# Retention and gated feed-forward on one core: the transposes of three more units by DMA, and one weight slice moved

## The chip, the cores and the metric

The kernel runs on one core of a Trainium2 chip. A core has TensorE (PE, matmuls; PEld is its load of weights), VectorE (DVE), ScalarE (ACT), GpSimd (POOL) and SyncE (SP, which here only issues DMAs), and 16 DMA engines [...]. The metric is the device time of one execution in microseconds (us); lower is better.

## The reference

Two stages. The first is a retention recurrence for 4 batches, 8 heads, 768 positions and a head size of 64; the second is a feed-forward layer with a SiLU on 3072 tokens of width 512 with an inner width of 2048. What is computed is

```python
gamma = 1.0 - 2.0 ** (-5.0 - np.arange(H))
for t in range(S):
    state = gamma[None, :, None, None] * state + np.einsum('bhd,bhe->bhde', k[:, :, t], v[:, :, t])
    y[:, :, t] = scale * np.einsum('bhd,bhde->bhe', q[:, :, t], state)
...
x = np.ascontiguousarray(attn_out.transpose(0, 2, 1, 3)).reshape(B * S, H * D)
h = x @ w_in
g = h * (1.0 / (1.0 + np.exp(-h)))
return g @ w_out
```

## The kernel before

**Units and chunks.** The 768 positions are cut into 6 chunks of 128. A unit is one chunk of one batch (all 8 heads); unit n is chunk n // 4, batch n % 4, so there are 24. Four units make one chunk of x: 512 tokens by 512 features. For each unit `k` and `q` are needed with the positions along the partitions (as loaded: `kf`, `qf`) and with the features along the partitions (`kt`, `qt`): the latter are transposes. `stage_t` (L429) makes them on TensorE, four 128x128 transposes for `k` and four for `q` into PSUM (`kp`, `qp`, L436), which ScalarE copies out (L438). `stage_s` (L446) makes the sums k times v, `stage_a` (L456) the scores from `kt` and `qt`, `stage_y` (L491) the outputs; its second half, the state products, waits for a fence: a `token` written by GpSimd (L377).

**The DMA's way to the transpose.** For units from `FAR` on (17 to 23) `part_t` (L407) has GpSimd copy `q` and `k` into two 16-bit planes each (`qp`, `kp`, L412), `turn_t` (L416) lets SP issue a transposing DMA for each (`qw`, `kw`, L419), and `join_t` (L422) has ScalarE put the 16-bit halves together to `qt` and `kt` (L426).

**Products.** The first matmul of the layer is cut into (c, f): chunk c of x by slice f of 128 inner features. `product_in` (L643) makes it with 12 matmuls of 512 columns: eight into `ha`, four into `hb` (L650), since each factor is split in a high and a low part and one for the cross terms. Then ScalarE takes `ha` out of PSUM (L660), VectorE subtracts `hb` (L665), ScalarE applies the SiLU (L670), and `put_g` has SP write the result `g` to memory (L676). Three PSUM banks `h0` to `h2` go round among the `ha`, `hb` and, in `stage_t`, `kp`. The loop over `steps` (L918) runs the products in a fixed order, with pairs and triples of chunks first, then (2, 3) to (2, 7), the middle slices of chunks 0 and 1, the last four slices of both, (2, 8) to (2, 15), and chunks 3 to 5 slice by slice. The second matmul (L967, L975) follows when all are done.

**Visits.** The attention work is hung between products: `visit(m)` (L594) does for unit m the transposes, for m - 1 the sums and scores, for m - 2 the outputs, and then issues the loads of a unit further on. The list `at` (L906) puts the visits of units 14 to 17 behind the products (1, 15), (2, 9), (2, 11) and (2, 13), later ones behind every fourth product of chunks 3 and 4.

**Lists that defer work.** What is appended to `behind_copy` runs after ScalarE's next L660, what is appended to `behind_next` after VectorE's next L665; `taken_out[0]` is that L665.

**Weights.** The weights come as pairs of 32-bit words. `take_w` (L253) converts one slice: a load on SP, one pass on ScalarE (L196) and six on VectorE (L199 to L217); slices 0 to 15 are of w_in and are split at once into three parts (L120 to L128, with the buffer `wl`), slices 16 to 31 are of w_out and are stored to memory again (`store_w`, L280), read back in chunk 5 (`get_w`, L692) and split there (`w_out`, L700). The list `takes` (L897) says behind which products a slice is taken.

**Late x of chunk 2.** The outputs of chunk 2 are also written to memory, and read back by `late_y` (L583) into `yr` tiles that `late_x` (L588) splits: loads behind (0, 14) and (1, 12), splits behind (1, 12), (1, 14) and (1, 15).

**Order.** The order on TensorE is written out by hand everywhere. After L882 the other queues are ordered by the scheduler of the tile framework from the order of the program, and by `queue(ins)`, which lets what follows be issued after an instruction. A tag with `bufs` n is a set of n buffers; a new tile waits until the last reader of a free one is done. `kt` has 2, `qt` 3, `kf` 3, `qf` 2, `wl` 1.

Of the kernel before, what the change touches and what calls it, by code (L numbers as in the profile page):

```python
# [33 lines left out]
def kernel(  # L34
# [28 lines left out]
    nc = tc.nc  # L63
# [78 lines left out]
    FAR = 4 * B + 1  # L142
    early = {}

    def load(name, n):
        if n >= len(units):
            return
        c, b = units[n]
        src = {"k": k, "q": q, "v": v}[name]
        if n < EARLY:  # L150

            if n not in early:
                early[n] = wpool.tile([128, 3, H, D], FP32, tag=f"w{4 + n}", name=f"kqv_{n}")
            t = early[n][:, "kqv".index(name)]
        else:
            t = ld.tile([128, H, D], FP32, tag=f"{name}f", name=f"{name}f_{n}",
                        bufs=2 if name == "q" else 3)
        nc.sync.dma_start(out=t, in_=src[b, :, ds(c * C, C)].rearrange("h t d -> t h d"))
        kqv[name][n] = t
# [247 lines left out]
    def part_t(n):  # L407

        for name, (p, tag, bufs) in (("q", (ld, "kf", 3)), ("k", (one, "kt", 2))):
            src = kqv[name].pop(n) if name == "q" else kqv[name][n]  # L410
            t = p.tile([128, 2 * H * D], U16, tag=tag, name=f"{name}p_{n}", bufs=bufs)
            nc.gpsimd.tensor_copy(out=t.rearrange("p (w h d) -> p w h d", w=2, h=H),  # L412
                                  in_=src.bitcast(U16).rearrange("p h (d w) -> p w h d", w=2))
# [169 lines left out]
    def late_y(b):  # L583
        tag = ("kt", "qt")[b % 2]
        y_late[b] = one.tile([128, KIN, C], FP32, tag=tag, name=f"yr_{b}", bufs=2 + b % 2)
        nc.sync.dma_start(out=y_late[b], in_=y_dram[b])
# [11 lines left out]
    def halves(m):  # L598
# [22 lines left out]
        if first and m < FAR:  # L621
            scale_k(m)
# [3 lines left out]

        if FAR <= m < len(units):
            with queue(fenced[0]):
                part_t(m)
        for name in "kqv":  # L630
            for n in (m + 1, m + 2):
                if n >= EARLY and n == (m + 1 if name == "v" or n > FAR else m + 2):
                    load(name, n)
# [6 lines left out]

    pending = []
# [258 lines left out]
    takes += [(0, NF - 2), (2, half), (2, half + 2), (2, half + 4)]  # L900
    takes += [(3, f) for f in (0, 3, 7, 11, 14)]
    takes += [(4, f) for f in (3, 7, 11, 14)]
    takes += [(5, f) for f in (2, 5, 8)]
# [4 lines left out]
    for i, x in enumerate(at):  # L908
# [7 lines left out]
    far = {steps.index(x): EARLY + 6 + i for i, x in enumerate(at)  # L916
           if FAR <= EARLY + 6 + i < len(units)}
    for n, (c, f) in enumerate(steps):  # L918
        if n - 2 in far:
            behind_next.append(lambda m=far[n - 2]: scale_k(m))  # L920
        if n - 3 in far:
            behind_copy.append(lambda m=far[n - 3]: [join_t(name, m) for name in "qk"])
# [6 lines left out]
        if n - 1 in far:  # L929
            turn_t(far[n - 1])  # L930
# [96 lines left out]
```

## Time and profile before

| | |
|---|---|
| median of 3 runs | 623.08 us (619.96 to 623.37) |
| the profiled execution | 619.42 us, span 617.6 us |
| TensorE busy | 603.8 us (98%) |
| VectorE, ScalarE busy | 422.9 us (68%), 313.0 us (51%) |
| GpSimd busy | 22.6 us (4%) |
| DMA queue of SP | 101.21 MB, 57.5% of 16 engines |

The span runs from the first to the last instruction of the trace. Busy shares are means over stages that differ: the first 97 us hold the early visits with little else to fill TensorE, then come products with and without visits up to 352 us, then the second matmul.

```profile
q1 hardware_dynamic: 135056, 101.21, 57.5%
HBM read 66.06 MB, written 36.70 MB: 166 GB/s over the span
L501 PE MATMUL y<-qt,mid 64*64 64x64 f32 x384 | 20.2, 224 | 1.0 <-POOL token L377 1.0
```

The first line gives packets, MB and the share of the 16 engines for SP's queue, the third a group of instructions: what it writes and reads, how many, busy time, mean duration, and the idle time before them with what ended it.

### The profile page before, as it was taken

To read this page: it belongs to the slowest core of one execution; us is meant where nothing else is said; L and a number is where in the kernel's file an instruction comes from. 1 tells how busy PE (TensorE), PEld (TensorE's weight loads), DVE (VectorE), ACT (ScalarE), POOL (GpSimd) and SP (SyncE) were. 2 spreads that over 40 slices of the span, in tenths; PEclk is the share of its full clock that TensorE was granted. 3 is DMA by queue.
4 is the path that set the end of the run, shared out by engine and by line. 5 is a ranking of instruction groups with operands and counts; after the bars stand their busy time and mean duration, and the time that the engine had idled before them with its cause. 6 is when DMAs were issued, how large, how long until landed. Compare 5 with 4: busy or idle time off the path is not lost.

```text
span 617.6 us, 13494 instructions
## 1 busy us (share of the span) xinstructions
PE 603.8 (98%) x5384; PEld 497.5 (81%) x5384; DVE 422.9 (68%) x731; ACT 313.0 (51%) x595; POOL 22.6 (4%) x79
## 2 busy tenths in 40 slices
PE   6899999999999999999999999999999999999997
PEld 5777887888888888888788888888888888888886
DVE  4998889899789877676699773635545453654631
ACT  6678896676654667766587732312221221412311
POOL 3000000000001111120000000000000000000000
PEclk9999999999999999999999999999999999999999
DMA  9989896464677999989767542533524433442301
GB/s 191 225 203 228 243 240 200 157 198 157 222 177 208 259 255 239 259 223 282 255 230 248 203 139 68 171 102 100 173 69 134 140 103 102 141 132 89 116 1 68
DMA packets 137999, 107.31 MB, mean 174 GB/s; under 512 B 94801, under 2 KB 103249, under 8 KB 137937
## 3 DMA queue, kind: packets, MB, share of 16 engines
q1 hardware_dynamic: 135056, 101.21, 57.5%
q10 hardware_dynamic: 2880, 5.24, 2.3%
q8 instruction: 42, 0.69, 0.5%
q14 instruction: 21, 0.16, 0.1%
HBM read 66.06 MB, written 36.70 MB: 166 GB/s over the span
## 4 chain that ended last, share of the span: by engine, by line
PE 84%; DVE 0%; DVEq 0%; issue 0%; POOLq 0%
PE ha L650 25%; PE o L967 21%; PE oa L967 14%; PE hb L650 12%; PE ob L967 7%; PE y L501 2%; PE sc L462 1%; PE sc L452 1%; PE o L975 0%; PE oa L975 0%; PE qp L436 0%; PE kp L436 0%; PE ob L975 0%; DVE o L993 0%; DVEq L1022 0%
## 5 line engine op out<-in xcount | busy, mean ns | idle before, releaser
L650 PE MATMUL ha<-xt,wi 128*128 128x512 f32 x768 | 193.8, 394 | 1.3 <-ACT xt L557 0.7
L650 PEld LDWEIGHTS ha<-xt,wi 128*128 128x128 f32 x768 | 141.9, 188 | 33.6 <-ACT wi L126 1.2
L967 PE MATMUL o<-wo,gs 128*128 128x512 f32 x564 | 143.2, 389 | 0.0
L717 DVE TENSOR_TENSOR gs<-gr,gs 128x512 fp32r<-128x512 f32 x96 | 62.1, 685 | 90.3 <-ACT gs L715 90.3
L967 PEld LDWEIGHTS o<-wo,gs 128*128 128x128 f32 x564 | 105.9, 188 | 21.9
L715 ACT ACTIVATE gs<-gr 128x512 fp32r<-128x512 f32 x96 | 53.6, 621 | 134.2 <-issue 131.8
L967 PE MATMUL oa<-wo,gs 128*128 128x512 f32 x376 | 115.8, 389 | 0.0
L650 PE MATMUL hb<-xt,wi 128*128 128x512 f32 x384 | 102.9, 390 | 0.0
L665 DVE TENSOR_TENSOR g<-g,hb 128x512 f32<-128x512 f32 x96 | 65.6, 683 | 42.0 <-ACT g L660 26.3
L650 PEld LDWEIGHTS hb<-xt,wi 128*128 128x128 f32 x384 | 71.8, 188 | 15.5 <-DVE g L665 0.2
L670 ACT ACTIVATE g<-g 128x512 f32<-128x512 f32 x96 | 60.3, 628 | 47.1 <-DVE g L665 47.1
L967 PEld LDWEIGHTS oa<-wo,gs 128*128 128x128 f32 x376 | 70.6, 188 | 14.7
L967 PE MATMUL ob<-wo,gs 128*128 128x512 f32 x188 | 73.7, 392 | 0.0
L660 ACT ACTIVATE g<-ha 128x512 f32<-128x512 f32 x96 | 57.0, 594 | 31.9 <-PE ha L650 15.1
L718 DVE SCALAR_TENSOR_TENSOR gs<-gs 128x512 fp32r<-128x512 f32 x96 | 62.0, 683 | 0.0
L967 PEld LDWEIGHTS ob<-wo,gs 128*128 128x128 f32 x188 | 35.3, 188 | 8.7 <-DVE o L985 1.6
L196 ACT ACTIVATE ca<-wf 128x512 f32<-128x512 f32 x32 | 21.4, 668 | 6.0 <-DVE cw L217 5.5
L212 DVE SCALAR_TENSOR_TENSOR ca<-wf,ca 128x512 f32<-128x512 uint32 x32 | 22.7, 710 | 0.5
L984 ACT ACTIVATE o<-o 128x512 f32<-128x512 f32 x10 | 6.0, 600 | 33.4 <-PE o L967 33.0
L206 DVE SCALAR_TENSOR_TENSOR cs<-ca,cs 128x512 uint32<-128x512 uint32 x32 | 22.1, 691 | 0.9
L501 PE MATMUL y<-qt,mid 64*64 64x64 f32 x384 | 20.2, 224 | 1.0 <-POOL token L377 1.0
L470 DVE TENSOR_TENSOR am<-sc,decay 128x512 f32<-128x512 f32 x24 | 16.5, 687 | 6.6 <-PE sc L462 6.5
(93 smaller groups left out, 562.0 us busy)
## 6 DMA issues: line engine op xcount, KB each, us to landing
gd<-g SPq DMA_DIRECT2D x96, 256.0 KB, 3.1
gr<-gd SPq DMA_DIRECT2D x96, 256.0 KB, 2.7
wf<-in_moe_w_out_dram SPq DMA_DIRECT2D x16, 512.0 KB, 4.2
out_dram<-o ACTq DMA_DIRECT2D x20, 256.0 KB, 2.1
wf<-in_moe_w_in_dram SPq DMA_DIRECT2D x16, 256.0 KB, 4.2
wf<-in_moe_w_in_dram SPq DMA_DIRECT2D x32, 128.0 KB, 4.0
kf<-in_k_dram SPq DMA_DIRECT2D x16, 256.0 KB, 5.1
qf<-in_q_dram SPq DMA_DIRECT2D x16, 256.0 KB, 4.0
```

The source lines that it names most:

```text
L196: nc.scalar.activation(out=a.bitcast(FP32), in_=hi.bitcast(FP32), func=AF.Abs, scale=65536.0)
L206: nc.vector.scalar_tensor_tensor(out=s, in0=a, scalar=3, in1=s, op0=ALU.logical_shift_left, op1=ALU.bitwise_or)
L212: nc.vector.scalar_tensor_tensor(out=p.bitcast(FP32), in0=lo, scalar=2.0 ** -52, in1=p.bitcast(FP32), op0=ALU.mult, op1=ALU.mult)
L501: i = nc.tensor.matmul(yp[ts(e, D), o, a, :], lhsT=lhsT, rhs=rhs, start=(e, o) not in started, stop=True, skip_group_check=True).ins
L650: nc.tensor.matmul(hb if i == 2 else ha, lhsT=w_sb[f][:, i, ts(kk, 128)], rhs=xt[c][:, i, kk, :], start=kk == 0 and i != 1, stop=kk == KIN ...
L660: copied[:] = [nc.scalar.activation(out=hs, in_=ha, func=AF.Copy, scale=ONE_E).ins]
L665: taken_out[:] = [nc.vector.tensor_tensor(out=hs, in0=hs, in1=hb, op=ALU.subtract).ins]
L670: nc.scalar.activation(out=hs, in_=hs, func=AF.Silu)
L715: nc.scalar.activation(out=t[:, 0, :], in_=g, func=AF.Copy, scale=HALF)
L717: nc.vector.tensor_tensor(out=t[:, 1, :], in0=g, in1=high, op=ALU.subtract)
L718: nc.vector.scalar_tensor_tensor(out=t[:, 2, :], in0=t[:, 1, :].bitcast(FP32), scalar=-1.0 / EPS, in1=high, op0=ALU.mult, op1=ALU.add)
L967: nc.tensor.matmul(o, lhsT=g, rhs=wo[f][:, i, :], start=f == 0 and i != 1, stop=f == NF - 1 and i != 0)
```

## The change

Three things. `FAR` becomes 14, so units 14 to 16 also leave `stage_t`: they are parted, turned and joined (`LATER`, 17, is where the old rhythm begins). Unit 14 is parted in the product (2, 3), turned after (2, 5), joined in (2, 8); units 15 and 16 are parted one visit ahead, turned a product after that, and joined in (2, 10) and (2, 12), where the old rhythm parts a unit in its own visit and joins it three products later. The loads of `k` and `q` of unit 15 and of `q` of 16 get places of their own (`apart`, `loads_at`), and `k` of 16 goes to `wl`; those of `k` and `q` of 17 are issued one visit later. The odd `late_y` tiles go to `wl` in place of `qt`. And the entry (2, 8) leaves the list of takes while (5, 0) joins it, so that the w_out slices after the first are each taken one place later, the thirteenth at (5, 0).

```diff
--- before.py
+++ after.py
@@ -139,7 +139,8 @@
     kqv = {"k": {}, "q": {}, "v": {}}
     EARLY = 2 * B
 
-    FAR = 4 * B + 1
+    FAR = 3 * B + 2
+    LATER = 4 * B + 1
     early = {}
 
     def load(name, n):
@@ -147,6 +148,11 @@
             return
         c, b = units[n]
         src = {"k": k, "q": q, "v": v}[name]
+        if n == LATER - 1 and name == "k":
+            t = conv.tile([128, H, D], FP32, tag="wl", name=f"kf_{n}")
+            nc.sync.dma_start(out=t, in_=src[b, :, ds(c * C, C)].rearrange("h t d -> t h d"))
+            kqv[name][n] = t
+            return
         if n < EARLY:
 
             if n not in early:
@@ -404,13 +410,17 @@
 
     planes, turned = {}, {}
 
-    def part_t(n):
+    def part_t(n, after=None):
 
         for name, (p, tag, bufs) in (("q", (ld, "kf", 3)), ("k", (one, "kt", 2))):
             src = kqv[name].pop(n) if name == "q" else kqv[name][n]
             t = p.tile([128, 2 * H * D], U16, tag=tag, name=f"{name}p_{n}", bufs=bufs)
-            nc.gpsimd.tensor_copy(out=t.rearrange("p (w h d) -> p w h d", w=2, h=H),
-                                  in_=src.bitcast(U16).rearrange("p h (d w) -> p w h d", w=2))
+            i = nc.gpsimd.tensor_copy(
+                out=t.rearrange("p (w h d) -> p w h d", w=2, h=H),
+                in_=src.bitcast(U16).rearrange("p h (d w) -> p w h d", w=2)).ins
+            if after is not None:
+                tc.add_manual_dep(i, after.name, mybir.DependencyInfo(
+                    mybir.DependencyClass.Sync, mybir.DependencyReason.DATA), reason="later")
             planes[name, n] = t
 
     def turn_t(n):
@@ -581,8 +591,8 @@
     y_late = {}
 
     def late_y(b):
-        tag = ("kt", "qt")[b % 2]
-        y_late[b] = one.tile([128, KIN, C], FP32, tag=tag, name=f"yr_{b}", bufs=2 + b % 2)
+        p, tag, bufs = ((one, "kt", 2), (conv, "wl", 1))[b % 2]
+        y_late[b] = p.tile([128, KIN, C], FP32, tag=tag, name=f"yr_{b}", bufs=bufs)
         nc.sync.dma_start(out=y_late[b], in_=y_dram[b])
 
     def late_x(b):
@@ -618,18 +628,20 @@
             if m > 3 * B + 1 and units[m - 1][1] == B - 1:
 
                 behind_copy.append(next_chunk)
-        if first and m < FAR:
+        if first and m < LATER:
             scale_k(m)
         if last:
             states_with(1)
             finish_y(m - 2, yp)
 
-        if FAR <= m < len(units):
+        n = m if m >= LATER else m + 1
+        if FAR < n < len(units) and (m < LATER - 1 or m >= LATER):
             with queue(fenced[0]):
-                part_t(m)
+                part_t(n)
         for name in "kqv":
             for n in (m + 1, m + 2):
-                if n >= EARLY and n == (m + 1 if name == "v" or n > FAR else m + 2):
+                if (n, name) not in apart and n >= EARLY and n == (
+                        m + 1 if name == "v" or n >= LATER else m + 2):
                     load(name, n)
         if EARLY + 2 <= m < 3 * B + 2:
             with queue(masked[0]):
@@ -638,6 +650,7 @@
                     begin_w()
 
 
+    apart = [(FAR + 1, "k"), (FAR + 1, "q"), (FAR + 2, "q")]
     pending = []
 
     def product_in(c, f):
@@ -897,10 +910,10 @@
     takes = [(1, 5)] + [(0, f) for f in range(6, half)]
     takes += [(2, half - 4), (2, half - 2)]
     takes += [(0, half), (0, half + 3), (1, half + 1), (1, half + 3)]
-    takes += [(0, NF - 2), (2, half), (2, half + 2), (2, half + 4)]
+    takes += [(0, NF - 2), (2, half + 2), (2, half + 4)]
     takes += [(3, f) for f in (0, 3, 7, 11, 14)]
     takes += [(4, f) for f in (3, 7, 11, 14)]
-    takes += [(5, f) for f in (2, 5, 8)]
+    takes += [(5, f) for f in (0, 2, 5, 8)]
     behind = {x: lambda: next(half_visits) for x in pairs[:-1]}
     behind[pairs[-1]] = lambda: [visit(3 * B + 1), behind_next.append(end_w)]
     at = ([(1, NF - 1)] + [(2, f) for f in range(NF - 7, NF - 2, 2)] +
@@ -913,21 +926,32 @@
     behind[1, NF - 1] = lambda: [late_x(3), visit(EARLY + 6)]
 
 
-    far = {steps.index(x): EARLY + 6 + i for i, x in enumerate(at)
-           if FAR <= EARLY + 6 + i < len(units)}
+    far = {m: steps.index(x) for m, x in enumerate(at, EARLY + 6)}
+    first_far = steps.index((2, 3))
+    parts = {first_far: FAR}
+    turns_at = {first_far + 2: FAR, far[FAR] + 1: FAR + 1, far[FAR + 1] + 1: FAR + 2}
+    joins_at = {far[m] + 1: m for m in range(FAR, LATER)}
+    for m in range(LATER, len(units)):
+        turns_at[far[m] + 1], joins_at[far[m] + 3] = m, m
+    scales_at = {far[m] + 2: m for m in range(LATER, len(units))}
+    loads_at = {first_far + 4: [("k", FAR + 1), ("q", FAR + 1)], far[FAR] + 1: [("q", FAR + 2)]}
     for n, (c, f) in enumerate(steps):
-        if n - 2 in far:
-            behind_next.append(lambda m=far[n - 2]: scale_k(m))
-        if n - 3 in far:
-            behind_copy.append(lambda m=far[n - 3]: [join_t(name, m) for name in "qk"])
+        if n in scales_at:
+            behind_next.append(lambda m=scales_at[n]: scale_k(m))
+        if n in joins_at:
+            behind_copy.append(lambda m=joins_at[n]: [join_t(name, m) for name in "qk"])
+        if n in parts:
+            behind_next.append(lambda m=parts[n]: part_t(m, taken_out[0]))
         product_in(c, f)
         put_g(1)
         store_w()
         if (c, f) in takes:
             take_w(taken_out[0], n < len(pairs + three))
         behind.get((c, f), lambda: None)()
-        if n - 1 in far:
-            turn_t(far[n - 1])
+        if n in turns_at:
+            turn_t(turns_at[n])
+        for name, m in loads_at.get(n, ()):
+            load(name, m)
         if c == NC - 1:
             if f == 0:
                 for i in range(W_READ):
```

## The prediction

> **What bounds the kernel now.** The head of the page first: which engine is full, and where.
>
> ```profile
> PE 603.8 (98%) x5384; PEld 497.5 (81%) x5384; DVE 422.9 (68%) x731; ACT 313.0 (51%) x595; POOL 22.6 (4%) x79
> ...
> PE   6899999999999999999999999999999999999997
> PEclk9999999999999999999999999999999999999999
> ```
>
> TensorE is busy for 98% of the span, and from the fourth slice on the row shows nothing but nines, at full granted clock. A busy row alone doesn't prove a bound, so the next view is what TensorE waited for after 97 us:
>
> ```profile
> PE ha L650 <- ACT wi L126: 0.4, 1, 0.4
> PE y L501 <- POOL token L377: 0.3, 1, 0.3
> ```
>
> That is 0.7 us in 520. So after the first 97 us the end is set by the number and length of TensorE's own instructions; other engines matter only once they become so late that it waits. The chain of waits gives each instruction's share of the path. Columns: start, length, what. First the visit of unit 16 (with transposes), then that of unit 17, which has its transposes from the DMA already:
>
> ```profile
> 187.45 0.44 PE kp L436 x4
> 187.89 0.44 PE qp L436 x4
> 188.33 0.86 PE y L501 x48
> ...
> 190.12 0.23 PE y L501 x16
> 190.35 2.04 PE ha L650 x8
> ...
> 196.02 0.86 PE y L501 x48
> 196.88 0.47 PE sc L452 x32
> 197.34 0.47 PE sc L462 x32
> 197.81 0.23 PE y L501 x16
> 198.04 2.04 PE ha L650 x8
> ```
>
> Both visits do the same work from `y` to the last `y` (0.86 + 0.47 + 0.47 + 0.23 = 2.03 us); that of unit 16 has 0.44 + 0.44 us of transposes before it. The whole visits are 190.35 - 187.45 = 2.90 and 198.04 - 196.02 = 2.02 us, so a unit's eight transposes cost 0.88 us of path. The groups give `kp` 276 and `qp` 273 ns each, 2.2 us a unit; those are latencies that overlap, so the chain is the row to price with.
>
> [...] beside unit 17's copy (1504 ns instead of a median 1051) two VectorE operations took 1.41 us each in place of 0.69. [...] here `kw` lands in a median 3.6 us, plain `kf` loads in 5.1.
>
> **The change part by part.** *Transposes of units 14 to 16 leave TensorE.* 3 x 0.88 = 2.6 us off the path. The clean length of a product stays 2.72 us (1.81 + 0.91). Nothing else on TensorE changes. Gain 2.6 us.
>
> *What takes their place.* Per unit two GpSimd copies, two DMA transposes on SP, two 16-bit joins on ScalarE in place of two PSUM copies.
>
> ```profile
> L426 ACT COPY kt<-kw 128x1024 uint16<-128x1024 uint16 x7 | 9.5, 1353 | 0.1
> L438 ACT COPY kt<-kp 128x512 f32<-128x512 f32 x17 | 9.8, 577 | 2.4 <-PE kp L436 2.4
> ```
>
> ```profile
> kw<-kp SPq DMA_TRANSPOSE x7, 3.6
> ```
>
> ScalarE: 2 x (1.36 - 0.58) = 1.55 us more a unit. Is there room? The windows from visit to visit (columns: length, busy PE, PEld, DVE, ACT, POOL, clock, DMA share, GB/s):
>
> ```profile
> 170.32:178.89 8.57, 8.57 (x162) 7.32 (x161) 6.95 (x14) 5.34 (x10) 0.09 (x1) 1.00 0.67 157
> 178.89:187.45 8.56, 8.56 (x162) 7.32 (x161) 7.93 (x16) 4.60 (x8) 0.09 (x1) 1.00 0.84 230
> 187.45:196.02 8.57, 8.57 (x165) 7.10 (x165) 7.94 (x16) 5.64 (x12) 0.09 (x1) 1.00 0.76 230
> ```
>
> Each window shrinks to 8.56 - 0.88 = 7.7 us. ScalarE becomes 6.9, 6.2, 7.2: it fits. DMA: a transpose is 256 KB like a load, and a load's 1024 packets of 18 ns are 1.15 us of the 16 engines (estimate: the same for a transpose). The loads of `k`, `q`, `v` are also spread otherwise, and I count about 7 us in each window: 90%, like the 0.93 of later windows where TensorE doesn't wait. VectorE: a `w_out` slice is 0.42 + 0.42 + 0.69 + 0.42 + 0.71 + 0.73 = 3.4 us. The slice that leaves (2, 8) ran from 177.5 to 182.4, in the first two windows; only the third stays at 7.9 for 7.7 us, so VectorE falls behind by 0.25 us there. An `hb` may be taken out up to 2.72 - 0.68 = 2.0 us after its end, before the product after next wants its bank; unit 16's was 0.6 late (188.03 against 187.45). So hidden, unless the copies slow VectorE as above (0.7 to 1.4 us a unit).
>
> *Is each unit's join in time?* I shift the trace by 0.88 us a visit. Unit 14: parted at (2, 3), turned at (2, 5), over 50 us (some 20 products) early; its loads of `k` and `q` of unit 15 follow at (2, 7). Join at (2, 8): ScalarE takes `ha` out at 174.4 and joins until 177.7; the scores need it at 179.4. Unit 15: parted after the fence at 171.5; SP turns `q`, then `k`, whose `qt` buffer comes free with the join of 14 at 177.7; lands by 181.5 (183.4 with the longest landing, 5.7); joined by 185.4, needed at 187.1. Unit 16: its `q` is loaded only after that transpose, issued about 179.4, landed 183.4 (median 4.0). GpSimd copies until 185.6, and is then free for the fence of visit 16 at 187; SP turns `k` from 186 (1.3 us of SP a transpose), landed by 190.5; at (2, 12) ScalarE takes `ha` out at 190.4, scales `gq` (1.27) and joins until 194.4. The scores of 16 start at 194.75. Slack 0.35 us: the tightest place. Behind GpSimd's copies stands the `token` of the next fence, and TensorE's state products wait for that; behind SP's transposes stand `gd` writes, whose `g` buffers ScalarE needs three products later. Below 0 is excluded (a wait can't gain); the upper bound, with every longest landing and copy (5.8, 1.25, 1.55, 5.7 us), is a fence 0.8 and a join 0.4 us late. I take 0.2 us.
>
> *`k` of 16 and odd late `y` tiles in `wl`.* That buffer's last reader before is the third part of the last `w_in` slice (to 156.8); `yr_1` then lands by 160.7 and is first wanted at 161.8. `yr_3` waited for the same reader before. Nothing, cover 1 us.
>
> *The slice at (5, 0).* Slices 1 to 12 are converted one place later, with their load, store and one ScalarE pass (0.67); the last of them is stored 20 us before it is read back. Chunk 5 gets 3.4 us of VectorE:
>
> ```profile
> 319.00:327.00 8.00, 8.00 (x37) 6.59 (x36) 8.00 (x16) 6.55 (x12) 0.00 (x0) 1.00 0.71 235
> 343.00:351.90 8.90, 8.90 (x41) 7.38 (x40) 5.88 (x10) 5.51 (x10) 0.00 (x0) 1.00 0.71 251
> ```
>
> VectorE is full from 309 to 335, so this isn't free: 8.00 of 8.00 us. But what is pushed back is first the splitting of weights and `gs`, which can wait until 351.9; the last window has 3.0 us free and 335 to 343 another 0.7. The products' own `hb` is already up to 1.7 us late of the 2.0 allowed. Bounds 0 and 1.5 us (half of the slice in front of the `hb`s); I take 0.2.
>
> Sum: -2.6 + 0.2 + 0.2 = -2.2 us on the profiled 619.42 (617.6 span and 1.8 around it): 617.2. That execution lies 3.7 us under the median of the runs, 623.08. With the same distance the forecast is 620.9.
>
> **Rivals.** *A little more.* If also the 0.7 us of waits and the slow first `ha` after a visit (2.04 for 1.81, three times 0.23) went: -2.6 - 0.7 - 0.7 = -4.0, 619.1. For it: less VectorE in chunk 2. Against: both waits lie elsewhere, and the small products still precede that `ha`.
>
> *Half given back.* GpSimd slows VectorE by 1.4 us beside the copies of units 15 and 16 each: an `hb` is then 0.6 + 0.25 + 2.8 late, less the 0.56 us that VectorE was idle at 184.8, 3.1 in all and 1.1 past its 2.0. With 0.2 + 0.2 the gain is 1.1 us: 622.0. For it: unit 17's copies did this. Against: those of 18 and 19 didn't.
>
> *Slower: the chain of unit 16 misses.* If `k` of unit 15 gets a `qt` buffer that comes free only with visit 15 (180.05) instead of the join, all behind it on SP moves by 2.4 us: `q` of 16 lands at 185.8 to 187.6, GpSimd is busy to 188.0 to 190.4, and the fence of visit 16 is up to 2.9 late; the transposes start then, and the join ends up to 2.5 later still against visit 17. Stalls of 5.4 us: 619.42 - 2.6 + 5.4 = 622.2, median 625.9. It decides the sign from 2.6 us of stall on. For it: three queues in series, 0.35 us slack. Against: it takes the late buffer and long landings at once.
>
> **How the numbers follow.** What a measurement of this kernel tells from no change is about 0.5%, 3.1 us. Forecast 0.55, a little more 0.10, half 0.15, slower 0.20. The forecast is -0.36%: with the play of the runs a bit under half of it counts as faster (0.26), the rest as within (0.28, 0.01 slower). A little more: faster, 0.10. Half: within, 0.15. Slower: 0.05 within, 0.15 slower. Sum 0.36, 0.48, 0.16. The range goes from 617 (the largest gain, and a lower draw of runs that lie 619.96 to 623.37) to 625.5, which leaves out the worst of the last case.
>
> **What would show it.** Right: visits 14 to 16 of 2.0 us on the chain with no `kp`, `qp`; products of 2.72 through (2, 15); no new wait of TensorE over 0.5 us. Wrong: TensorE waiting for the `token` or a joined `qt`/`kt` at visits 16 and 17, or for `hb` in chunks 2 or 5; VectorE operations of 1.4 us beside GpSimd's copies.

## The result and the profile after

The changed kernel takes 623.56 us (median; 621.15 to 627.77) against 621.51 us for the kernel before on the same chip (619.76 to 623.68): a ratio of 1.0033, 95% interval 1.0018 to 1.0049. It is 2.1 us slower, where 2.2 us of gain were forecast, though the transposes are gone from TensorE as planned.

The head of the page of the changed kernel, the same rows as before:

```profile
PE 603.4 (97%) x5360; PEld 496.0 (80%) x5360; DVE 423.4 (68%) x731; ACT 316.7 (51%) x595; POOL 29.1 (5%) x85
...
PEclk9899999999999999999999999999999999999999
```

24 of 5384 matmuls are missing (3 units, 8 transposes), GpSimd has its six copies more (79 to 85), and the share of TensorE has gone down while the span has grown by 3.6 us. (The 8 in the second slice of the clock is a granted clock of one half from 26.6 to 30.0 us. The repeat and the version with only the slice moved have such a stretch there too (mean granted clock 0.996 and 0.997, as 0.997 here); the trace before has none (1.000). By 97 us the products start 2.0 us later than before, ahead of anything that the change touches. What is compared below is therefore the work from 97 us on.) What TensorE waited for after 97 us, where there were two waits of together 0.7 us before:

```profile
PE sc L472 <- ACT kt L436: 2.0, 3, 1.2
PE ha L663 <- ACT wi L126: 0.4, 1, 0.4
PE ha L663 <- DVE g L678: 0.4, 1, 0.4
PE y L511 <- POOL token L383: 0.3, 1, 0.3
PE y L511 <- DVE xt L570: 0.2, 1, 0.2
```

The first line is new: three times the scores waited for a `k` that ScalarE had not joined yet. Where, the starts of TensorE's products show. I subtract them between the two traces, product by product; each difference stays constant as long as nothing happens, and steps where something does:

| place | step, us | what the trace has there |
|---|---|---|
| visit 14 | -0.88 | no `kp`, `qp` |
| visit 15 | -0.61 | no `kp`, `qp`; 0.2 waited for `xt` |
| visit 16 | -0.88 | no `kp`, `qp` |
| visit 17 | +0.67 | waits 0.44 for `kt` of unit 16 |
| visit 18 | +1.48 | waits 1.2 for `kt` of unit 17 |
| visit 21 | +0.58 | waits 0.3 for `kt` of unit 20 |
| (5, 5) to (5, 7) | +1.11 | `ha` waits for `g` (VectorE's `hb`) |
| second phase | 0.1 | |

The sum is +1.5 us: 2.4 gained, 3.8 lost. The medians differ by 2.1 us, with an interval of 1.1 to 3.0; the 0.6 us between the two are not traced. The chain of waits of the changed kernel (start, length, what) shows the gain and the two largest losses among the joins. Visit 14 first:

```profile
172.23 0.86 PE y L511 x48
173.09 0.47 PE sc L462 x32
173.55 0.47 PE sc L472 x32
174.02 0.23 PE y L511 x16
174.25 2.04 PE ha L663 x8
...
182.75 1.05 POOL kp L418
183.80 0.02 issue
183.83 0.70 DVE kf L404
...
191.28 0.70 DVE cw L223
191.98 0.02 issue
192.00 0.05 ACT ca L202
...
194.72 1.36 ACT qt L436
196.09 1.20 ACT kt L436
...
202.26 7.05 DMA qw<-qp
209.31 0.02 issue
209.33 1.37 ACT qt L436
210.71 1.20 ACT kt L436
211.90 0.04 issue
211.95 0.69 PE sc L472 x32
```

The visit is 2.02 us long, as priced. Then the chain leaves TensorE, which it did not do before. At 182.75 it runs through GpSimd's copy of unit 16 into VectorE's scaling of that `k` (L404), a whole queue of VectorE, the `ca` pass of a slice and the join of unit 16. At 202.26 it is a DMA transpose of unit 17, in flight for 7.05 us. Unit 17 was transposed by the DMA before as well; there the same transfer took 4.6. ScalarE's own rows for its joins, before:

```profile
207.04 1.37 ACT L426 COPY qt<-qw 128x1024 uint16<-128x1024 uint16 x1 [0.49 <-DMA qw<-qp]
208.29 1.35 ACT L426 COPY kt<-kw 128x1024 uint16<-128x1024 uint16 x1
```

and after:

```profile
209.33 1.37 ACT L436 COPY qt<-qw 128x1024 uint16<-128x1024 uint16 x1 [1.74 <-DMA qw<-qp]
210.57 1.32 ACT L436 COPY kt<-kw 128x1024 uint16<-128x1024 uint16 x1
```

`k` of unit 17 is whole at 211.9 instead of 209.6. Before, the first of these scores started at 210.29: 0.65 us of slack. A delay of 2.26 less 0.65 less the 0.22 by which TensorE came later leaves 1.4 us, nearly all of the step of 1.48. (The view of the waits counts only from the end of the matmul before, hence its 1.2.)

Why does it take 7 us? The first part is SP's issue. Before and after:

```profile
202.39 1.67 SPq L419 DMA_TRANSPOSE qw<-qp  x1
202.26 3.02 SPq L429 DMA_TRANSPOSE qw<-qp  x1
```

So 1.35 us of the 2.4 were lost before SP had issued the transfer, at 205.28. What goes with that is other traffic. The load of a weight slice (512 KB) was issued 2.6 us ahead of the transpose and landed 2.3 us after the start of its issue; before, it was 3.3 us ahead and landed 0.9 us after. In the first 2 us of the issue, packets of 2 and 4 KB (the slice and the stores) moved 528 KB, against 285 KB before. The second part, from the end of the issue to the landing, is 4.03 us instead of 2.96. The windows of one microsecond in the changed kernel (columns: length, busy PE, PEld, DVE, ACT, POOL, clock, DMA share, GB/s):

```profile
206.00:207.00 1.00, 1.00 (x6) 0.81 (x6) 0.00 (x0) 0.01 (x1) 0.00 (x0) 1.00 0.78 142
207.00:208.00 1.00, 1.00 (x6) 0.84 (x5) 0.38 (x1) 0.59 (x1) 0.00 (x0) 1.00 2.66 168
208.00:209.00 1.00, 1.00 (x7) 0.80 (x5) 0.98 (x3) 0.00 (x0) 0.00 (x0) 1.00 0.07 8
209.00:210.00 1.00, 1.00 (x47) 0.70 (x49) 0.95 (x2) 0.67 (x1) 0.00 (x0) 1.00 1.16 355
```

From 208 to 209 the DMA moves 8 GB/s, in the middle of a transpose that is not done. The queues of the DMA between 207 and 209 us of the same run:

```profile
q1 hardware_dynamic: 654, 0.16, 132.9%
q8 instruction: 1, 0.02, 3.6%
```

One packet of 16 KB on the instruction queue, begun at 207.1, takes 1.15 us of one of the 16 engines (3.6% of 16 x 2 us). The small packets of the transposes are 256 B and take a median 18 ns; 21 of them took 1.25 to 1.5 us beside it, and the rest of the transfer only went on when they were through, at 209.0; the large packet had ended at 208.2. There are 42 such packets in an execution, and TensorE runs 2 x 5360 matmuls and weight loads, 255 for each packet (before 2 x 5384, 256 for each); two versions below with 416 and 208 instructions more have 44 and 43. From this count and the queue's name I take them for its instructions, and call such a packet a fetch. The one at 207.1 is the 22nd of the execution; before the change the 22nd came at 200.0, and SP issued the transpose at 202.4.

These windows show the packet and the stop together, and no more: small packets also stopped at 205.3 to 206.6 in this trace, and for 1 us at 243.1 in the trace before, with no 16 KB packet near. A count over all transposes is stronger. The 20 traces of this case hold 362 with a known landing. Of the 66 with a 16 KB packet between the end of the issue and the landing, 27 took more than 3.5 us for that stretch; of the 296 without one, none did. What the packet can account for here is that stretch, 1.07 us; it began 1.8 us after the long issue was over.

### The profile page after: what moved, and what is told of

Read it like the earlier page. It is cut to its first block, busy times and chain, and to the rows that moved or that the text cites. A ratio compares the mean times of both kernels' runs of the same rounds, so it can differ in the third digit from the quotient of the medians.

```text
span 621.2 us, 13462 instructions
## 1 busy us (share of the span) xinstructions
PE 603.4 (97%) x5360; PEld 496.0 (80%) x5360; DVE 423.4 (68%) x731; ACT 316.7 (51%) x595; POOL 29.1 (5%) x85
## 4 chain that ended last, share of the span: by engine, by line
PE 74%; DVE 3%; DMA 2%; ACT 2%; issue 1%; POOL 0%; SPq 0%; DVEq 0%; POOLq 0%
PE o L991 21%; PE ha L663 20%; PE oa L991 14%; PE hb L663 10%; PE ob L991 7%; DMA qw<-qp 2%; PE y L511 1%; PE sc L472 1%; ACT qt L436 1%; ACT kt L436 1%; DVE g L678 1%; DMA kw<-kp 1%; PE o L999 0%; DVE cw L223 0%; PE sc L462 0%
```

## The experiments

Steps are again by the products' starts against the kernel before; ratios are against the kernel before, run beside it. Theory: three different waits, one for each loss, and the largest is a collision of TensorE's instruction fetch with the transposes of unit 17. Rivals: the DMA traffic or SP's queue behind the added transposes; GpSimd slowing VectorE.

**Repeat, and the slice alone.** The changed kernel again; then the kernel before with nothing but

```
-    takes += [(0, NF - 2), (2, half), (2, half + 2), (2, half + 4)]
+    takes += [(0, NF - 2), (2, half + 2), (2, half + 4)]
...
-    takes += [(5, f) for f in (2, 5, 8)]
+    takes += [(5, f) for f in (0, 2, 5, 8)]
```

and the changed kernel with that taken back.

> The changed kernel once more, for a second trace. Theory (chains): TensorE waits again for a joined kt at the visits of units 17 (0.4 us) and 18 (1.2 us) and again about 0.6 us at the visit of unit 21, and loses 1.1 us in chunk 5. Rival (chance): the 7.05 us landing of qw of unit 17 was one slow transfer; then visits 18 and 21 show no wait and only chunk 5 and visit 17 repeat. The dip of the clock in the second slice (0.8) is expected to be absent or elsewhere.

> The kernel before with only the weight slice moved from (2, 8) to (5, 0). Theory (chunk 5 pays): +1.1 us, products at (5, 5) and (5, 6) of more than 2.72 us because an hb is taken out late; ratio 1.0018. Rival (chunk 5 hides it): 0, ratio 1.000, products all 2.72 us.

> The changed kernel with the slice back behind (2, 8): all three units by DMA. Theory (chains and chunk 5): chunk 5 gives its 1.1 us back, the waits at visits 17, 18, 21 stay: about +0.6 us over the kernel before, ratio 1.001. Rival (the slice had to leave chunk 2): VectorE passes its window in chunk 2, hb comes late there, and 2 us or more are lost: ratio 1.003 or above. Second rival (all from the slice): the waits at visits 17, 18 and 21 go with it and the full 2.6 us show: ratio 0.996.

The repeat (624.38 us) has nearly the same steps: -0.88, -0.84, -0.88, +0.67, +1.73 and +1.5 in chunk 5. Visit 21 differs, with +0.1, and the product (2, 8) loses 0.61, for which visit 15 keeps more: `hb` waits 0.26 us for `xt` there. The half clock in the second slice, which I expected gone, is there again. The slice alone costs +0.55, +0.31 and +0.13 us at (5, 5) to (5, 7), 1.0 in all, and nothing elsewhere; the ratio, 1.0004 (0.9986 to 1.0021), is too coarse for it. The window of that run:

```profile
318.00:329.00 11.00, 10.62 (x46) 8.08 (x45) 11.00 (x20) 9.59 (x18) 0.00 (x0) 1.00 0.92 292
```

VectorE has no free time (11.00 of 11.00), and now TensorE has (10.62). With the slice back at (2, 8), chunk 5 costs nothing, but chunk 2 pays: visit 16 loses 0.52 instead of gaining 0.88 (0.9 us of wait for `xt` from VectorE), and visits 17, 18, 20 and 21 lose 0.72, 1.72, 0.69 and 0.95. That adds up to +3.1 us in this trace, while the ratio, 1.0008 (0.9982 to 1.0035), is worth 0.5: the steps of a single trace can be far from the median. The move of the slice and that of the transposes belong together: with transposes gone, VectorE has 2.6 us less for the same work.

**Fewer units, and the scaling of `k` of unit 16.** Units 14 and 15 by the DMA, unit 16 on TensorE, the slice as before (first diff, its core); and the changed kernel with the second.

```
+    LAST = 15
...
-        if first and m < FAR:
+        if first and (m < FAR or LAST < m < LATER):
             stage_t(m)
...
-    joins_at = {far[m] + 1: m for m in range(FAR, LATER)}
+    joins_at = {far[m] + 1: m for m in range(FAR, LAST + 1)}
```

```
-        if first and m < LATER:
+        if first and m < LATER - 1:
             scale_k(m)
...
+    scales_at[far[LATER - 1] + 1] = LATER - 1
```

> Units 14 and 15 by DMA, unit 16 back on TensorE, k and q of 17 loaded a visit earlier again, the slice as before. Theory (the chain of 16 and what it pushes onto 17 costs): visits 14 and 15 are 0.88 us shorter each, no waits at 17, 18 and 21: -1.8 us, ratio 0.997. Rival (any added transposes crowd the DMA queues): the waits at 18 and 21 stay, -1.8 + 2.0: ratio 1.000.

> The changed kernel with the scaling of k of unit 16 tied to the product (2, 12). Theory (VectorE's order): VectorE no longer sits idle for 2.5 us behind GpSimd's copy of k of 16, the slice of (2, 10) ends earlier, ScalarE's next ca pass doesn't hold up the join of 16, and the wait at visit 17 goes from 0.67 us to under 0.2. Rival (the DMA chain of unit 16 itself is late: q loaded after the transpose of 15): the wait at visit 17 stays. Visit 18 and chunk 5 as in the changed kernel.

With two units, visits 14 and 15 gain 0.88 and 0.82, visit 17 waits for nothing, and visit 18 still loses 1.19, against what I expected and as the rival had it, with `k` and `q` of unit 17 loaded as early as before. The ratio of 1.0041 (1.0021 to 1.006) comes from elsewhere: the second phase is 3.6 us longer, with three waits that the changed kernel hasn't:

```profile
PE oa L994 <- ACT o L1011: 2.4, 3, 1.0
```

With the scaling one product later, visit 17's step is 0.00 instead of +0.67. VectorE's queue shows why. In the changed kernel it stands still until GpSimd has copied `k` of unit 16, with the work of visit 15 and a slice behind it:

```profile
180.62 0.68 DVE L678 TENSOR_TENSOR g<-g,hb 128x512 f32<-128x512 f32 x1
183.83 0.70 DVE L404 TENSOR_TENSOR kf<-kf,gk 128x512 f32<-128x512 f32 x1 [2.53 <-POOL kp L418]
184.44 0.69 DVE L480 TENSOR_TENSOR am<-sc,decay 128x512 f32<-128x512 f32 x1
```

The scaling overwrites the tile that the copy reads, so it must wait; in the run with the edit it stands at 194.90, and nothing waits. The rest stays (+1.31 at visit 18): 623.49 us.

**Moving the fetches by a count.** If a fetch comes with every 255 or 256 instructions, as counted, idle matmuls on TensorE should bring every later one to an earlier place in the work. First 24 of them ahead of all work in the changed kernel, 104 in the kernel before, and a combination of three mends:

```
+    fill = const.tile([64, 64], FP32, tag="fill", name="fill")
+    nc.vector.memset(fill, 0.0)
+    into = banks("q", "filled", 1)
+    for _ in range(24):
+        nc.tensor.matmul(into[:64, 0, :64], lhsT=fill, rhs=fill, start=True, stop=True,
+                         skip_group_check=True)
```

> The changed kernel with 24 idle 64x64 matmuls at its start, while TensorE waits for its first constants: 48 more instructions in TensorE's stream, as many as the transposes of three units took out. They compute nothing that is used. Theory (instruction fetch): the 16 KB packets, one for every 256 instructions of TensorE, come at the places in the work at which they came in the kernel before; none lies within qw of unit 17 any more (qw lands in about 4.7 instead of 7 us), the wait at visit 18 goes from 1.25 to under 0.3 us, also that at visit 21. The wait at visit 17 (0.67) and chunk 5 (1.1) stay. Net -1.2 us against the changed kernel, ratio 1.000 to 1.001. Rival (the transposes crowd the DMA queues, or the loads of 17 come too late): the wait at visit 18 stays at 1.2 to 1.7 us.

> The kernel before with 104 idle matmuls at its start: 208 instructions, the same shift modulo 256 as the 48 that the change takes out. Theory (instruction fetch): a 16 KB packet falls some 5 us later than the one at 200 us and into qw of unit 17, which then lands in 6 us or more, and TensorE waits about 0.5 to 1.5 us at visit 18, with no transpose moved at all. Rival: no wait at any visit, as in the kernel before.

> All three remedies: 24 idle matmuls at the start, the scaling of k of 16 behind (2, 12), and the slice that left (2, 8) put behind (4, 9) in place of (5, 0). Theory: visits 14 to 16 are 0.88 us shorter each, no waits at 17, 18 and 21, chunk 5 all at 2.72 us; -2.3 us, ratio 0.9965. Rival (the DMA queues are too full for three more units): a wait of 1 us or more stays at visits 17, 18 or 21, ratio 0.999 or above.

The count was wrong in all three: such a matmul in FP32 is two matmuls and two weight loads in the trace, so that 24 are 96 instructions and 104 are 416. The fetches of the kernel with 104 therefore didn't stand where the test wanted them; it waits for nothing at visit 18, has none in its transposes of unit 17, and starts its products 19.5 us later. It tells little. In the two others visit 18 has no wait, as expected, but visit 17 lost 1.39 and 1.80 us (and visit 16 of the first 0.68, waiting for `xt`). In the first it waited 0.49 us for `kt` and was slow for the rest; in the second TensorE stood still in the middle of the visit, with nothing that it waited for in the trace:

```profile
PE y L511 <- issue: 1.5, 1, 1.5
```

A visit runs 2 x (48 + 32 + 32 + 16) = 256 matmuls and weight loads in 2 us, a whole packet's worth, where a product runs 24 in 2.72 us; a fetch that came late is one reading of the stop (it is from 202.1 to 203.6 us, the packets are at 201.1 and 204.6), which was not tested by itself. The ratios are 1.0087 (1.0068 to 1.0107) and 1.0066 (1.0049 to 1.0084); the slice at (4, 9) in the second cost 0.72 us, and nothing in chunk 5.

Then the count kept: four idle matmuls in each of visits 14 to 16 in the place of the eight transposes; with the later scaling and the slices of chunk 5 at 0, 3, 6 and 9; and 52 idle ones in the kernel before, ahead of visit 14.

```
         if first and m < FAR:
             stage_t(m)
+        elif first and m < LATER:
+            idle(4)
...
-    takes += [(5, f) for f in (0, 2, 5, 8)]
+    takes += [(5, f) for f in (0, 3, 6, 9)]
...
         product_in(c, f)
+        if steps.index((2, 8)) - 13 <= n < steps.index((2, 8)):
+            idle(4)
```

(`idle(n)` is the loop above with n matmuls; the second edit is in the run with three mends only, the third in the kernel before only.) With them ran the kernel with two units again, with `turns[0] += 2` ahead of the second phase.

> The changed kernel with four idle 64x64 fp32 matmuls (8 matmul and 8 weight-load instructions) in each of visits 14, 15 and 16, in the place of the eight transposes that the change took out, so that every later instruction of TensorE has the number it had before. Nothing is left out of the computation. Theory (instruction fetches): TensorE's 16 KB fetch falls back to some 200 us, ahead of the 16-bit transposes of unit 17, qw of unit 17 lands in some 5 us instead of 7, and the wait of 1.2 us at visit 18 and the step of 0.6 us at visit 21 go; 0.67 us at visit 17 (the late scaling of k of unit 16) and 1.1 us in chunk 5 (the slice) stay. The idle matmuls cost 0.1 to 0.5 us a visit. Sum against before by the products' starts: -2.6 + 0.9 + 0.3 + 0.7 + 1.1 = +0.4, against +1.4 for the changed kernel: ratio about 1.000. Rival (the transposes of units 14 to 16 themselves push those of unit 17 back in SP's queue): the wait at visit 18 stays at 1.0 us or more and qw of unit 17 still takes 7 us.

> As the run with the kept count, and in addition the scaling of k of unit 16 is put one product later, as for the later units, and the slices of chunk 5 stand at its products 0, 3, 6 and 9 instead of 0, 2, 5 and 8. Nothing is left out. Theory: visits 14 to 16 save 0.7 us each less 0.3, visits 17, 18 and 21 add nothing, and chunk 5 adds 0.3 us or less if its cost is two slices only two products apart: -1.5 to -2.2 us against before, ratio 0.9965 to 0.998. Rival for chunk 5 (a fourth slice there costs what it costs, whatever its place): 1.0 us stays, ratio about 0.999.

> The kernel before with 52 idle 64x64 fp32 matmuls (208 TensorE instructions, four after each of the 13 products ahead of visit 14), so that its later fetches fall 48 instructions (256 less 208) later in the work, as in the changed kernel, though no transpose is moved. Nothing is left out. Theory: up to 7 us more ahead of visit 14 from the idle matmuls; then a fetch falls inside qw of unit 17, which takes some 7 us, and TensorE waits 1 us or more for it at visit 18. Rival (SP's queue behind the added transposes): no wait at visit 18, qw of unit 17 lands in 4.7 us as before.

> The run with units 14 and 15 by the DMA and unit 16 on TensorE, with the rotation of the three accumulators set forward by two ahead of the second phase, so that it begins on the bank it had before. Nothing is left out. Theory: the 3.5 us that the second phase had more go (261.8 us again), and the rest stays: -0.88, -0.82, 0 and +1.2 at visit 18, so -0.5 us against before, ratio 0.998 to 1.000. Rival (the second phase was longer for the DMA's sake): it stays at 265 us, ratio 1.004.

With the count kept the fetch comes at 202.7, ahead of the transpose (205.1); the join starts 5.1 us after the issue, and visit 18 loses 0.51 instead of 1.48. It isn't 0: the fetch now falls into SP's issue of the load of `k` before it, which took 1.49 us (0.42 in the changed kernel), and `qw` was issued 0.7 later behind the product (2, 15) than before. Ratio 1.0009 (0.9988 to 1.003): half of each visit's gain goes to the idle matmuls (-0.43). With the two more mends visit 17 adds nothing, but a fetch fell 1.2 us into the transposes, in SP's issue of `qw`, which then landed after 6.2 us, and visit 18 lost 1.25; the four slices of chunk 5 cost 1.4 us at these places too. Ratio 1.0019 (1.0001 to 1.0037). In the kernel before, shifted, a fetch came 4.7 us after the issue, `kw` was late instead, and visit 18 lost 0.36 where it never had: less than the 1 us expected, with no transpose moved at all. The fourth run contradicts what I held of the run with two units: with the accumulators turned back the second phase is as long (1.0047; 1.0028 to 1.0065). What ScalarE waited for ahead of the output tiles, in that run (us, times), names another buffer:

```profile
  DMA out_dram<-o: 7.0, 3
```

The output tiles share buffers with `kt` and `qt`; how many of these a version has taken by then decides whether an output waits for the store of one before. That was read from the trace and not tested.

**Moving the transposes.** Instead of the fetch, the transposes of units 17 to 23 were moved: issued right after the visit, ahead of the slice's store and the next store of `g`. One run with that alone, one with the two other mends alone, one with all three (the diff of the slice: `(4, f) for f in (3, 7, 11, 12, 14)` and `(5, f) for f in (2, 5, 8)`).

```
-        turns_at[far[m] + 1], joins_at[far[m] + 3] = m, m
+        turns_at[far[m]], joins_at[far[m] + 3] = m, m
...
-        store_w()
+        early = turns_at.get(n, 0) >= LATER
+        if not early:
+            store_w()
...
+        if early:
+            store_w()
```

> The changed kernel with the 16-bit transposes of units 17 to 23 issued one product earlier, right after the visit of the unit, ahead of that product's store of a w_out slice and of the next store of g in SP's queue. Nothing is left out. Theory (the wait at visit 18 is one of the DMA side: SP's queue, the transposes and the 16 KB fetches among them): qw of unit 17 issues at some 200 us instead of 202.3, lands at 206 to 207 even with a fetch in it, and the waits at visits 18 and 21 go; 0.67 us at visit 17 and 1.1 us in chunk 5 stay: -2.4 + 0.7 + 1.1 = -0.6 us by the products' starts, ratio 0.998 to 1.001. Rival (the join is late because ScalarE or VectorE are, with TensorE 2 us ahead of them): qw lands earlier and the wait at visit 18 stays over 1.0 us.

> The changed kernel with the scaling of k of unit 16 one product later and the moved slice at the product (4,12) instead of (5,0), ahead of the only stretch of chunk 4 in which VectorE has a whole product's time idle (2.85 us in the trace of the kernel before). Nothing is left out. Theory: visit 17 adds nothing, the slice adds 0 to 0.7 us at (4,13) to (4,15) and nothing in chunk 5; 1.3 us at visit 18 and 0.6 at visit 21 stay: -2.4 + 0.3 + 1.3 + 0.6 = -0.2 us, ratio 0.998 to 1.001.

> Both: the transposes of units 17 to 23 issued earlier, the scaling of k of unit 16 later, and the slice at (4,12). Nothing is left out. Theory: what remains is the gain of the three visits, -2.4 us, and up to 0.7 for the slice: -1.7 to -2.4 us against before, ratio 0.996 to 0.998. Rival (something else is late by the same amount as soon as TensorE gains 2 us): the total by the start of the second phase is within 0.5 us of before, ratio 0.999 to 1.002.

The move is a failure: 1.0134 (1.0099 to 1.017), and 1.0119 (1.0093 to 1.0146) with the others. SP's queue and ScalarE in the first of them:

```profile
202.26 3.84 SPq L429 DMA_TRANSPOSE qw<-qp  x1
206.20 1.26 SPq L429 DMA_TRANSPOSE kw<-kp  x1
207.55 1.77 SPq L286 DMA_DIRECT2D wod<-cw  x1
209.41 1.51 SPq L689 DMA_DIRECT2D gd<-g  x3
```

```profile
212.13 0.60 ACT L673 ACTIVATE g<-ha 128x512 f32<-128x512 f32 x1 [5.03 <-DMA gd<-g]
```

The transpose now stands 0.5 us behind the load of `k` and 0.9 behind that of a slice of 512 KB, and took SP 3.84 us to issue; three stores of `g` stood behind, and ScalarE waited 5 us for a free `g` buffer. Visit 18 lost 4.43, some of it at a granted clock of one half from 213.5 to 216.9 us. It can't tell the theory from its rivals.

The two other mends alone keep what they promised: visits -0.88, -0.53, -0.88, nothing at visit 17, +1.38 at visit 18, nothing at 21, and nothing for the slice, which, taken behind (4, 12), is ahead of VectorE's only idle product, (4, 14) (0.00 us busy from 302.6 to 305.4 in the trace before). Ratio 0.9996 (0.9981 to 1.0012).

**One variable.** That last kernel with 8, 12 and 18 idle matmuls ahead of all work, by the same lines as above. (The texts for 8 and 18 refer to the one for 12.)

> The same with eight idle matmuls (32 instructions). Nothing is left out. Theory: the fetch falls some 3.5 us earlier than in the run without them, at 202 us, about the issue of qw: SP's issue of it is lengthened to 2.5 us or more, the join starts 5.2 to 6.5 us after the issue, and 0.5 to 1.3 us of wait at visit 18 stay. Ratio 0.997 to 1.000. Rival: as with twelve, no dependence on the number.

> The run with the later scaling of k of unit 16 and the slice at (4,12), with twelve idle 64x64 fp32 matmuls (48 TensorE instructions) ahead of all work, while TensorE waits for its first inputs. Nothing is left out. From visit 17 on the fetches stand where they stood before the change. Theory (fetches): the one of 205.6 us falls at some 200, ahead of the transposes of unit 17; qw's join starts 5.2 us or less after its issue instead of 6.3, the wait at visit 18 is 0 to 0.5 us instead of 1.4, and no visit is starved by more than 0.5: -1.5 to -2.2 us over the products from 97 us on, ratio 0.996 to 0.999 (the start may cost up to 1 us). Rival (the place of the fetch is an accident of the slow runs, not their cause): a wait of 1 us or more stays at visit 18.

> The same with eighteen idle matmuls (72 instructions). Nothing is left out. Theory: the fetch falls well ahead of the transposes, within or close behind visit 17; the join starts 5.2 us or less after the issue and visit 18 waits 0 to 0.3 us, but visit 17 may be starved of instructions by 0.5 to 1.8 us, as with 96 instructions. Ratio 0.997 to 1.001. Rival: a wait of 1 us or more stays at visit 18.

Here are all runs whose transposes of unit 17 are issued at the old place. The columns in the middle are read from the 16 KB packets (the nearest one that starts ahead of the join), SP's queue and ScalarE's first join of unit 17, in us from the start of the issue of `qw`; "rest" is from the end of the issue to the start of the join:

| run | 16 KB packet | SP issues `qw` in | join starts at | rest | step at visit 18 |
|---|---|---|---|---|---|
| before | -2.4 | 1.67 | 4.7 | 3.0 | 0 |
| slice alone | -2.7 | 1.68 | 4.6 | 3.0 | 0 |
| 24 idle | -1.6 | 2.63 | 5.2 | 2.6 | 0 (visit 17 late) |
| combination of three | -3.0 | 2.05 | 4.7 | 2.7 | 0 (visit 17 late) |
| 104 idle, before | -4.4 | 2.14 | 4.7 | 2.5 | 0 |
| count kept | -2.4 | 2.44 | 5.1 | 2.6 | +0.51 |
| 18 idle | -3.2 | 1.56 | 4.3 | 2.7 | +0.21 |
| changed | +4.8 | 3.02 | 7.1 | 4.1 | +1.48 |
| repeat | +5.0 | 3.22 | 7.3 | 4.1 | +1.73 |
| slice back | +4.4 | 2.57 | 6.7 | 4.1 | +1.72 |
| two units | +4.2 | 2.25 | 6.3 | 4.1 | +1.19 |
| two units, turned | +4.1 | 2.36 | 6.4 | 4.0 | +1.22 |
| later scaling | +4.1 | 2.25 | 6.3 | 4.0 | +1.31 |
| scaling and slice | +4.1 | 2.50 | 6.3 | 3.8 | +1.38 |
| 8 idle | +5.1 | 2.57 | 7.1 | 4.5 | +2.66 |
| 12 idle | +1.0 | 3.81 | 6.4 | 2.5 | +1.40 |
| three mends | +1.2 | 3.62 | 6.2 | 2.6 | +1.25 |
| before, 52 idle | +4.7 | 2.26 | 4.8 (`kw` late) | 2.5 | +0.36 |

In ten traces a packet falls 1 to 5 us after the issue and the join starts at 6.2 or later; all ten lose more than 1 us at visit 18. In seven it comes 1.6 us or more ahead of the issue, the join starts at 4.3 to 5.2, and they lose 0 to 0.51. The last row is apart: the packet came as `qw` landed, and `kw` was late.

The ten are of two kinds. In eight the packet falls behind the issue, and the rest is 3.8 to 4.5 us where it is 2.5 to 3.0 in all others. In two (12 idle, three mends) it falls into the issue, which is then the longest of the table, and the rest is short. There `hb` of the product ahead of the visit waits 0.6 and 0.4 us for ScalarE, before the scores wait 0.3 for `kt`.

The length of the issue goes with other traffic too. In the 16 traces with no 16 KB packet in it, it took 1.56 to 2.26 us in the six where packets of 2 and 4 KB moved 258 to 285 KB in its first 2 us, and 2.25 to 3.22 in the ten where they moved 385 to 547 KB. So of the rivals, the traffic on the DMA engines is not excluded for this half of the delay; no run varied it alone.

The runs with 8, 12 and 18 idle matmuls differ in nothing but that number. Eight and twelve failed what I expected of them: the packet did not come where the count put it (+5.1 and +1.0, not about 0 and ahead), and the wait came with the packet. (With eight, 1.9 of the 2.66 are the wait; from 213.7 to 217.1 us the granted clock was one half, and the product (3, 2) lost another 1.03.) With eighteen it came at 198.8, 3 us ahead of the transpose:

```profile
201.93 1.56 SPq L429 DMA_TRANSPOSE qw<-qp  x1
203.58 1.41 SPq L429 DMA_TRANSPOSE kw<-kp  x1
```

```profile
206.20 1.36 ACT L436 COPY qt<-qw 128x1024 uint16<-128x1024 uint16 x1 [0.30 <-DMA qw<-qp]
207.43 1.36 ACT L436 COPY kt<-kw 128x1024 uint16<-128x1024 uint16 x1
```

The join starts 4.3 us after the issue, visits 14 to 16 keep their 3 x 0.88, and visit 18 adds 0.21. Its waits after 97 us:

```profile
PE sc L472 <- ACT kt L436: 0.8, 2, 0.5
PE y L511 <- POOL token L383: 0.3, 1, 0.3
PE ha L663 <- ACT wi L126: 0.3, 1, 0.3
```

The first line is now at visits 20 and 21 (+0.56, +0.72). This version is faster than the kernel before: 620.47 us against 623.50 beside it, ratio 0.996 (0.9944 to 0.9975). With twelve it is 0.9972 (0.9949 to 0.9996), with eight 1.0002 (0.9979 to 1.0026). The steps from 97 us on explain the differences among the three, but not all of the 3.0 us: they add up to -1.1 (-2.6 + 0.2 + 0.6 + 0.7), -0.5 and +1.2 us, and each median is 1.6 to 2.0 us lower than that. What a few idle matmuls do for the start by themselves was not measured. In the executions with a granted clock of 1.000 the medians are 619.9 us (6 of 22) and 621.0 (8 of 43), 1.1 us apart, as traced.

## Why the prediction was wrong

- *Transposes of units 14 to 16, -2.6.* Right: 0.88 a visit, less only where something else was late (0.61 at visit 15 here) or idle matmuls took the place (0.43). "Nothing else on TensorE changes" was wrong in one respect: with 48 instructions fewer the 22nd fetch came at 207.1 us in place of 200.0, in a transfer with 0.65 us of slack.
- *What takes their place, +0.2.* The step that failed. It asked whether each added join comes in time and found unit 16's the tightest, at 0.35 us. The join of unit 16 was indeed late (+0.67), but by a way that wasn't looked at: its `k` was scaled one visit early and stopped VectorE for 2.5 us behind GpSimd's copy; with the scaling later it is in time. And the joins of units 17 and 20, which the change doesn't touch, weren't asked after: +1.48 and +0.58. For unit 17 the transfer was 2.4 us longer: 1.35 in SP's issue, which goes with denser traffic, and 1.07 behind it, with a fetch in it. The term measured 2.7 us, not 0.2.
- *GpSimd slows VectorE.* Small. Beside the copies of unit 15 two operations took 1.41 and 1.52 us in place of 0.69, and visit 15 kept 0.61 of its 0.88; in the repeat two such operations (1.55 and 1.41 us) cost 0.61 at (2, 8). The rival "half given back" put 1.1 us on it.
- *The slice at (5, 0), +0.2 of bounds 0 to 1.5.* Mis-sized: 1.0 alone, 1.1 in the change. VectorE being full there was seen; that the products' own `hb` would be pushed past its limit was priced too low.
- *`k` of 16 and odd late `y` tiles in `wl`, 0.* Nothing was seen of them.
- *The rival that ends slower* had the right kind (a join misses its visit by SP's and DMA's doing) and the wrong unit and reason: no wait for a `qt` buffer shows.

What stays open: the waits at visits 20 and 21 (0 to 0.95 us in the runs), and where a fetch will fall, which could not be computed from the count alone. In the changed kernel a packet fell into the issue of unit 20's `qw` (2.77 us). With eighteen idle matmuls none did (1.29), and visit 21 still lost 0.72: SP came to that transpose 6.4 us after the start of the product (3, 10), 3.1 in the kernel before, because the store of `g` ahead of it took until then; why is not traced further. That a fetch in the transposes goes with the wait is shown in 17 of the 18 traces of the table, and that a stretch of over 3.5 us behind the issue never comes without one in 362 transposes; whether it is the packet that stops them, and how, is not shown. Why SP's issue took 3.02 us instead of 1.67 is open: packets of 2 and 4 KB moved nearly twice as much beside it, and that was not tested by itself.

## What to carry to other kernels

Work taken off the bounding engine brings forward every deadline behind it (by up to 2.4 us here), so ask for the slack of all later joins, not only of those that were added, and for the order in which an in-place operation stands behind a reader on another engine (here VectorE stood still for 2.53 us behind GpSimd's copy). Among the data of this unrolled program 42 packets of 16 KB moved on the instruction queue; when a change of a few instructions makes a transfer elsewhere slow, look for the large packet on the instruction queue, and split the transfer at the end of its issue: what is lost ahead of that can have another cause than what is lost behind it. And before a slice of work is moved, look for a window in which the engine that does it is idle: the same slice cost 1.0 us in a full stretch, 0.7 at (4, 9) and nothing at (4, 12).

## What the runs showed of the hardware

- With a 16 KB instruction packet between the end of SP's issue and the landing, 27 of 66 DMA transposes of 1024 packets of 256 B needed more than 3.5 us for that stretch; without one, none of 296 did. In the changed kernel the DMA moved 8 GB/s for a microsecond there.
- SP's issue of a DMA transpose took a median 1.3 us where no such packet fell into it; with one in it, 32 of 57 issues took over 2 us (up to 4.3), without one 21 of 305. In the run with the transposes moved, the next issues stood behind one of 3.84 us: three stores of `g` were issued from 209.4 us on, and ScalarE waited 5.03 us.
- In the combination of three TensorE stood still for 1.5 us in a visit of small matmuls with no wait in the trace; why is not shown.
- An idle FP32 matmul of 64x64 counts as two matmuls and two weight loads: 104 of them are 208 and 208 in the trace, and with 18 the page has 5396 of each in place of 5360.
